# Even weight pieces through six places between two decoder layers, and two more key chunks parked in PSUM

## The chip, the cores and the metric

The kernel runs on one core of a Trainium2 chip. Its time is the device time of one execution in microseconds; the median of several executions is given. The profile is of one further execution.

## What is computed

Two layers, each an attention block over a cached sequence and a small mixer with an MLP, for two sequences (B = 2) with one new token each. In short:

```python
def _A_ref(x, k_cache, v_cache, wq, wo):        # H = 32 heads, Dh = 128, Sk = 16384
    q = heads(x @ wq)
    p = softmax(einsum("bhqd,bhkd->bhqk", q, k_cache) * Dh ** -0.5)
    return merge(einsum("bhqk,bhkd->bhqd", p, v_cache)) @ wo
def _B_ref(x, w1, w2, w3, w4):                  # D = 576, F = 4608; one token, so the shifts give zeros
    x1 = x + hs
    return x1 + gelu(layernorm(x1) @ w3) @ w4
x = x + _A_ref(layernorm(x), K, V, wq, wo)
x = x + _B_ref(layernorm(x), w1, w2, w3, w4)
# and both lines once more
```

Both layers use the same caches and weights. All inputs are bf16.

## The kernel before

**Tiles and places.** The keys and the values of one (sequence, head) pair, a unit, are 4 MB each: 128 partitions with 128 blocks of 128 elements. There are 64 units. A buffer `mem` holds six slots of 4 MB; `Store` (line 269) keeps which 128-byte-per-partition cells of it are in use. `plan` (line 278) appends a transfer with its place to one list; `pump` (line 286) issues the head of the list as soon as its cells have no owner, and stops at the first whose cells are still owned. `release` (line 322) frees the cells of a used piece and pumps again. So all transfers stand in one order on SP's queue, each waits there for the last reader of its place, and one that waits holds back all behind it. SP issues every transfer from line 101.

**A unit.** Half of a unit's key blocks go through PE: eight blocks at a time (a chunk) are transposed into one of four PSUM buffers `tps` (`transposes`, line 1219), copied by ACT to SBUF (`evacuate`, line 1233, instruction at line 1237) and multiplied with q as eight matmuls of one column (`scores`, line 1240, matmuls at line 1251). The other half goes through DVE (`dots`, lines 1271 and 1275), which needs q spread over the partitions (`q_broadcast`, line 1187). The softmax takes its maximum over the partitions on POOL (`softmax_max`, line 1278) and its exponentials on ACT (`softmax_exp`, line 1294); `pv` (line 1327) multiplies the values, 32 blocks at a time. Two loops of three units per turn hold most of it; the stretches around the loops are written out.

**Between the layers.** The last two units of layer 0 (62 and 63) stay in their slots, since layer 1 begins with them: four of the six slots. Their blocks that went through DVE in layer 0 are transposed in place while the weights come in, a chunk at a time, so that layer 1 can score them without a transpose: `turn` (line 1058) transposes a chunk, `settle` (line 1068) has ACT copy it back. Sixteen chunks are turned: four at the start of the last unit (line 967), ten at the places listed in `TURNS` (line 344), two after the w3 product. The unit before them, 61, also stays in part: `park` (line 1073) transposes its first three key chunks (`PARKED`) into the three SBUF buffers `kt`, which frees their place, and the first 72 of its 128 value blocks (`GONE`) are given up and loaded again for layer 1.

The weights wo, w3, w4 and the next wq, some 20 MB, come through what is free: four places of 4608 bytes per partition in the slot of unit 61's values (`A`, lines 524 to 542) and one in the slot of its keys (`B`), where the three parked chunks were. A place holds a piece of 576 KB. Most pieces are of that size; rows 1 and 2 of w3 (by blocks of 128 rows) are 1152 KB in two neighbouring places, the first of wq is 1024 KB, and w4 has two of 288 KB. `rows_projection` (line 859, matmuls at line 872) multiplies wo and w4 piece by piece, `cols_chunk` (line 740, matmuls at line 751) and `cols_tail` (line 759, line 768) w3 and wq; each frees its piece and then turns chunks as `TURNS` says, and `turn` settles them at once unless told otherwise.

Between the products stand the residual sum (line 850), two layernorms (line 684: totals over the partitions by a matmul at line 695, a square root on ACT at line 707, the reciprocal at line 711), the spreading of the last rows (line 725), the GELU (line 909) and the layernorm ahead of wq. The first product of w3 and of wq takes the unnormalized x and is corrected afterwards, so it doesn't wait for the layernorm; the later ones need `xn`.

After q (line 814) `carried` (line 1083) writes out the first three units of layer 1: scores of units 62 and 63 straight from `mem` (`still`), those of unit 61 from the parked chunks (`third`) and from fresh transposes (`fresh`), with dots, maxima and value products between them. Behind the weights the list has the value blocks of unit 61 given up before (four pieces of 576 KB), the keys of unit 0 in quarters, as those of unit 62 are scored, and then whole tiles.

Of the kernel before, what the change touches and what calls it, by code (L numbers as in the profile page):

```python
# [328 lines left out]
class KB:  # L329
# [100 lines left out]

    def plan_tile(self, t, u, slot, cuts=()):

        b, hh = u % self.B, u // self.B
        src = (self.K if t == "k" else self.V)[b, hh].rearrange("(p j) d -> p (j d)", p=128)
        cuts = [0, *cuts, self.NB]
        for a, z in zip(cuts[:-1], cuts[1:]):
            self.plan_piece(t, u, slot, src, a, z - a)

    def plan_piece(self, t, u, slot, src, a, n):
        sem = f"tile{slot}" if n == self.NB else f"piece{slot}_{a}_{n}"  # L440
        self.store.plan((t, u, a, n), sem, slot * self.TILE + 256 * a, 256 * n,
                        [(lambda m: m, src[:, a * 128:(a + n) * 128])])
# [60 lines left out]
    def plan_all(self):  # L503

        T, U, n = self.TILE, self.U, self.KT - 1
        row, w3r, wqr = 2 * self.D, 2 * self.F, 2 * 128 * self.H
        H, MT = self.H, self.MT
# [4 lines left out]
        tiles = self.tile_order(0)  # L512
# [3 lines left out]
        for (t, u), slot in zip(tiles, place):  # L516
# [15 lines left out]
        h = MT // 2  # L532
# [3 lines left out]
        h = H // 2  # L536
# [7 lines left out]
        tiles = self.tile_order(1)  # L544
        place = [(3, 4, 5, 0, 2, 1)[i % 6] for i in range(len(tiles))]
        for i, (t, u) in enumerate(tiles):
            if (t, u) != ("v", third):
                self.plan_tile(t, u, place[i], (quarter, half, half + quarter) if i == 0 else
                               (half,) if i == len(tiles) - 1 else ())
        self.cuts["wo", 1] = [(0, 11, 2 * T), (11, 22, 2 * T + 11 * row), (22, 32, 0)]  # L550
# [188 lines left out]

    def cols_chunk(self, w, l, k, out, pk, n, rhs, rk, cols, first, last=False):  # L740

        c = rhs.shape[-1]
        for i, (kk, lo, hi, _) in enumerate(self.parts[w, l]):
            if kk != k:
                continue
            nm = (w, l, i)
            buf = self.store.buf(nm)

            def f(pe, buf=buf, lo=lo, hi=hi):
                for m in range(lo, hi):  # L750
                    ins = pe.matmul(out[:, m * c:(m + 1) * c], lhsT=cols(buf, m, lo), rhs=rhs, start=first and m == 0,
                                    stop=last, skip_group_check=True)
# [41 lines left out]
    def q_projection(self, l):  # L794
# [6 lines left out]
        self.layernorm("x", self.x, self.xn, "xn",  # L801
                       after=lambda: self.cols_chunk("wq", l, 0, acc, [ak], n, self.raw[:, 0, 0:w], "raw", cols, True, True))
        be = self.coef[:, 1, :]
# [55 lines left out]
    def rows_projection(self, w, l, rhs, rk):  # L859
# [4 lines left out]
        for i, (a, b, _) in enumerate(cuts):  # L864
# [11 lines left out]
            self.store.release(nm)  # L876
            if l == 0:
                self.turn(self.TURNS.get((w, i), 0))

    def z_projection(self, l):  # L880
# [5 lines left out]
        cols = lambda buf, m, lo: self.cols4(l, buf, m)  # L886
        chunk = lambda k: self.cols_chunk("w3", l, k, acc, [ak], MT, self.raw[:, k, :], "raw", cols, k == 0, k == R - 1)
        chunk(0)
        self.layernorm("x1", self.x1, self.xn, "xn", after=lambda: chunk(1))
        self.spread_tail()  # L890
        al, be = self.coef[:, 0, :], self.coef[:, 1, :]
# [55 lines left out]
    def attention(self, l):  # L947
# [11 lines left out]
        for s in range(self.CARRY + 1 if l else 0, U):  # L959
# [6 lines left out]
            still = self.still(l, s)  # L966
            if still and s == U - 1:
                self.unturned = [(v, b) for v in o[U - self.CARRY:] for h in range(2)
                                 for b in range(h * self.BP + self.PB, (h + 1) * self.BP, self.CH)]
                self.unsettled = []  # L970
                self.turn(4)
            self.landed(l, "k", u, both=turning)
            after = self.early(l, s - 1)
            for c in range(2 * n):
# [24 lines left out]
                elif s >= 1:  # L999
# [5 lines left out]
                    if turning or s < U - 1:  # L1005
                        if c == n:
                            self.softmax_exp(l, s - 1, o[s - 1])
# [20 lines left out]
        if leave < U:  # L1028
            self.park(o[leave - 1])
        self.softmax_exp(l, s, u)  # L1030
# [41 lines left out]

    def park(self, u):

        n = self.PARKED
        self.store.carve(("k", u, 0, self.NB), [self.CH * (i + 1) for i in range(n)] + [self.BP])
        for c in range(n):
            self.transposes(0, u, c * self.CH, c, self.chunk)
            self.store.release(("k", u, c * self.CH, self.CH))
            self.unsettled.append((self.chunk, (None, self.kt[c][:, :, :].rearrange("p j n -> p (j n)"), [("kt", c)])))  # L1080
            self.chunk += 1

    def carried(self, o):
# [13 lines left out]
        def fresh(c):  # L1097
            self.transposes(1, o[2], c * self.CH, c, self.chunk)
            self.evacuate(c, self.chunk, (None, self.kt[c % self.NKT][:, :, :].rearrange("p j n -> p (j n)"),
                                          [("kt", c % self.NKT)]))  # L1100
            self.chunk += 1

# [16 lines left out]
        fresh(5)  # L1119
        still(1, 6, 11)  # L1120
        third(4)
        fresh(6)
        still(1, 11, N)
        self.softmax_max(1, 1, o[1])
        third(5)
        fresh(7)
        for g in range(2):
            self.pv(1, 0, o[0], g)
        third(6)
        dots(2)  # L1130
        for g in range(2, 4):
            self.pv(1, 0, o[0], g)
        third(7)
        self.softmax_exp(1, 1, o[1])
        dots(3)
        self.keep_o(1, 0)
        self.keep_l(1, 0)
        for g in range(4):
            self.pv(1, 1, o[1], g)
        self.q_broadcast(o[3], 3)  # L1140
# [300 lines left out]
```

## Time and profile before

| | |
|---|---|
| median of 3 runs | 2559.52 us (2559.41 to 2559.8) |
| the profiled execution | 2557.7 us |
| its span, from the first to the last instruction | 2556.0 us |
| busy: PE, DVE, ACT, POOL | 63%, 74%, 47%, 2% of the span |
| moved by DMA | 1093.19 MB, mean 428 GB/s |

The profile's page gives busy shares for 40 equal slices of the span, the chain of work that ended last, and the groups of instructions by line. Other views give the same for stretches (`from:to length, busy time of each engine with its instructions, granted clock, DMA share, GB/s`), the chain in order of time (`start, us, what`), the timeline (`start, us, engine line operation, in brackets the idle time before and who ended it`) and, for a line that issues transfers, the time from issue to landing. All times are microseconds from the start of the span.

### The profile page before, as it was taken

The page shows a single profiled execution, that of the slowest core. Times are in us where ns is not written, and L with a number is a line of the kernel's source. Part 1 is how long each engine was busy: PE and PEld are TensorE (multiplying, and loading weights), DVE is VectorE, ACT ScalarE, POOL GpSimd, SP SyncE. Part 2 cuts the span into 40 slices and gives each one's busy share as a digit, 9 for nine tenths or more (in the row PEclk, how much of TensorE's full clock was granted, in tenths as well). Part 3 has the DMA queues.
Part 4 walks back from the last instruction along what each step waited for, and adds up shares of the span by engine and source line. Part 5 has one row for each costly group of instructions (what it writes and reads, how often), then busy time and mean ns, then how long its engine had stood idle before and what let it go on. Part 6 is the DMA issues. An engine that isn't in the chain of part 4 may idle for free.

```text
span 2556.0 us, 74895 instructions
## 1 busy us (share of the span) xinstructions
PE 1616.7 (63%) x34407; PEld 1582.5 (62%) x34407; DVE 1899.1 (74%) x2074; ACT 1200.7 (47%) x1808; POOL 52.5 (2%) x151
## 2 busy tenths in 40 slices
PE   4666666666666666665777666666666666666566
PEld 3666666656656666665667656666665666666566
DVE  5877777777777777777648777777777777777774
ACT  3544444544444454444435544454444445444442
POOL 0000000000000000000000000000000000000000
PEclk8555555555555555555655555555555555555655
DMA  9999999999999999999999999999999999999999
GB/s 410 430 430 433 431 431 432 432 431 431 432 431 432 431 432 433 431 432 432 414 359 427 433 431 431 433 431 432 432 430 434 430 432 433 431 431 432 431 433 388
DMA packets 46496, 1093.19 MB, mean 428 GB/s; under 512 B 5092, under 2 KB 6248, under 8 KB 11624
## 3 DMA queue, kind: packets, MB, share of 16 engines
q1 hardware_dynamic: 46440, 1092.40, 99.9%
q8 instruction: 41, 0.67, 0.1%
q14 instruction: 15, 0.12, 0.0%
HBM read 1092.37 MB, written 0.00 MB: 427 GB/s over the span
## 4 chain that ended last, share of the span: by engine, by line
DMA 66%; DVE 22%; PE 5%; issue 5%; SPq 1%; ACT 1%; DVEq 0%; POOLq 0%
DMA mem<-in_A_k_cache_dram 64%; DVE s_dve L1275 12%; DVE prod L1271 8%; PE tps L1225 2%; PE mps L1345 2%; DMA mem<-in_B_w_dram 2%; SPq L101 1%; PE sps L1251 1%; DMA mem<-in_A_wq_dram 1%; PE sps L1196 1%; ACT mem L1237 0%; DVE diag L1192 0%; DMA mem<-in_A_wo_dram 0%; DVE q_col L1189 0%; DVE l L1323 0%
## 5 line engine op out<-in xcount | busy, mean ns | idle before, releaser
L1237 ACT ACTIVATE kt<-tps 128x1024 bf16<-128x1024 bf16 x992 | 1003.0, 1023 | 878.4 <-PE tps L1225 862.0
L1275 DVE TENSOR_REDUCE s_dve<-prod 128x16 f32<-128x2048 bf16 x504 | 1152.1, 2286 | 17.3
L1225 PE MATMUL tps<-ident,mem 128*128 128x128 bf16 x8192 | 1000.2, 300 | 140.1 <-POOLq L202 134.8
L1271 DVE TENSOR_TENSOR prod<-mem,qb 128x2048 bf16<-128x2048 bf16 x504 | 616.7, 1224 | 533.1 <-POOLq L202 498.1
L1345 PE MATMUL mps<-p,mem 128*128 128x1 bf16 x16384 | 512.1, 165 | 549.6 <-POOLq L202 522.5
L1225 PEld LDWEIGHTS tps<-ident,mem 128*128 128x128 bf16 x8192 | 762.7, 136 | 149.8 <-POOLq L202 144.3
L1345 PEld LDWEIGHTS mps<-p,mem 128*128 128x128 bf16 x16384 | 488.2, 105 | 557.3 <-ACT p L1306 553.7
L1251 PEld LDWEIGHTS sps<-q_col,kt 128*128 128x128 bf16 x7936 | 399.6, 113 | 0.7 <-issue 0.5
L1251 PE MATMUL sps<-q_col,kt 128*128 128x1 bf16 x7936 | 387.8, 170 | 0.6 <-issue 0.4
L1196 PE MATMUL sps<-diag,ones_bf 128*128 128x128 bf16 x127 | 36.5, 288 | 194.1 <-DVE diag L1192 194.1
L1196 PEld LDWEIGHTS sps<-diag,ones_bf 128*128 128x128 bf16 x127 | 13.3, 105 | 204.3 <-DVE diag L1192 204.3
L1300 ACT ACTIVATE mx<-mx 128x1 f32<-128x1 f32 x128 | 26.1, 204 | 233.6 <-POOL mx L1291 233.6
L1199 ACT ACTIVATE qb<-sps 128x128 bf16<-128x128 f32 x127 | 35.2, 277 | 139.2 <-PE sps L1196 139.2
L1291 POOL PARTITION_ALL_REDUCE mx<-mx x128 | 50.1, 392 | 2450.7 <-DVE mx L1289 2321.5
L1237 ACT ACTIVATE mem<-tps 128x1024 bf16<-128x1024 bf16 x32 | 31.3, 1043 | 33.1 <-PE tps L1225 28.0
L1303 ACT ACTIVATE p<-s_dve,mx 128x64 bf16<-128x64 f32 x126 | 43.8, 348 | 4.1
L1306 ACT ACTIVATE p<-sps,mx 128x64 bf16<-128x64 f32 x128 | 37.7, 294 | 0.1
L1286 DVE TENSOR_REDUCE mx<-sps 128x1 f32<-128x64 f32 x128 | 27.6, 216 | 7.5 <-PE sps L1251 7.5
L872 PE MATMUL mps<-prod,mem 128*128 128x2 bf16 x680 | 22.1, 166 | 17.2 <-DMA mem<-in_B_w_dram 7.0
L872 PEld LDWEIGHTS mps<-prod,mem 128*128 128x128 bf16 x680 | 20.2, 104 | 19.5 <-DMA mem<-in_B_w_dram 7.8
L1192 DVE TENSOR_SCALAR diag<-ident,q_f 128x128 bf16<-128x128 bf16 x127 | 31.1, 245 | 0.0
L707 ACT ACTIVATE misc<-misc 128x2 f32<-128x2 f32 x8 | 2.4, 294 | 52.4 <-DVE misc L705 52.4
(122 smaller groups left out, 293.1 us busy)
## 6 DMA issues: line engine op xcount, KB each, us to landing
mem<-in_A_k_cache_dram SPq DMA_DIRECT2D x124, 4096.0 KB, 40.7
mem<-in_A_v_cache_dram SPq DMA_DIRECT2D x123, 4096.0 KB, 49.6
mem<-in_B_w_dram SPq DMA_DIRECT2D x9, 1152.0 KB, 33.4
mem<-in_B_w_dram SPq DMA_DIRECT2D x17, 576.0 KB, 7.3
mem<-in_A_v_cache_dram SPq DMA_DIRECT2D x3, 2048.0 KB, 40.4
mem<-in_A_wq_dram SPq DMA_DIRECT2D x5, 1024.0 KB, 7.0
mem<-in_A_wo_dram SPq DMA_DIRECT2D x8, 576.0 KB, 18.6
mem<-in_A_wq_dram SPq DMA_DIRECT2D x8, 512.0 KB, 6.9
```

The lines of the kernel that those rows point to most:

```text
L872: ins = pe.matmul(self.mps[:, t * B:(t + 1) * B], lhsT=buf[:, o:o + 128], rhs=rhs(k), start=(k == 0 and t == 0), stop=(k == last), skip_gr ...
L1196: self.pe(lambda pe: pe.matmul(qps, lhsT=self.ones_bf[:, :], rhs=self.diag[:, :], start=True, stop=True, skip_group_check=True), reads=["o ...
L1199: self.act(lambda e: e.activation(out=self.qb[i][:, :], in_=qps, func=ACT.Copy), reads=[("qps", i)], writes=[("qb", i)], sig=("qb", i))
L1225: ins = pe.transpose(self.tps[t][:, j * 128:(j + 1) * 128], buf[:, j * 128:(j + 1) * 128], self.ident[:, :])
L1237: self.act(lambda e: e.activation(out=out, in_=self.tps[t][:, :], func=ACT.Copy), reads=[("tps", t)], writes=keys, sig=("evac", c, t, k))
L1251: ins = pe.matmul(self.sps[sp][:, c * self.CH + j:c * self.CH + j + 1], lhsT=buf[:, j * 128:(j + 1) * 128], rhs=self.q_col[:, sp:sp + 1], ...
L1271: self.dv(lambda e: e.tensor_tensor(out=prod, in0=buf.rearrange("p (j d) -> p j d", d=128), in1=qbc, op=ALU.mult), reads=[("qb", r)] + key ...
L1275: self.dv(lambda e: e.tensor_reduce(out=sd[:, c0:c0 + DB], in_=prod, axis=AX.X, op=ALU.add), reads=["prod"], writes=[("s_dve", r)], sig=(" ...
L1291: self.pool(lambda e: e.partition_all_reduce(mx[3], mx[2], channels=128, reduce_op=ROP.max), reads=[("mx2", i)], writes=[("mx3", i)])
L1303: self.act(lambda e: e.activation(out=p[:, n:self.NB], in_=self.s_dve[i][:, 0:self.NB - n], func=ACT.Exp, bias=mx[4], scale=self.scale, ac ...
L1306: self.act(lambda e: e.activation(out=p[:, 0:n], in_=self.sps[i][:, 0:n], func=ACT.Exp, bias=mx[4], scale=self.scale, accum_out=self.ls[:, ...
L1345: ins = pe.matmul(self.mps[:, 448:449], lhsT=buf[:, j * 128:(j + 1) * 128], rhs=p[:, col:col + 1], start=b == 0, stop=b == self.NB - 1, sk ...
```

## The change

1. **Six places, even pieces.** `PARKED` is 5. The two new parked chunks are transposed behind the second wo product and stay in two of the four PSUM buffers until layer 1 copies them; `self.full` names these buffers and `turn` and `fresh` pass over them. Their place in `mem` makes a second place `c[1]` beside `B`, now `c[0]`. All pieces of wo, w3, w4 and wq go through the six places in turn, and w3 and wq are cut into halves: w3 comes in nine pieces (seven before), wq in nine (eight before).
2. **Turns.** The four chunks that were turned at the start of the last unit are turned in the middle of the one before it. Of the ten in `TURNS` some stand behind other products. Chunks turned inside a layernorm (after the second w3 row and the first wq row) are settled only when the layernorm has been issued (`held`).
3. **The list behind the weights.** The first quarter of unit 0's keys goes to the place of the parked chunks instead of unit 62's slot and stands ahead of the last of unit 61's value pieces.
4. **Layer 1's first products.** In `carried` both units' scores come in a row; the dots, maxima, fresh transposes and value products follow in another order. Fresh transposes 3 and 4 drop out, since these chunks wait in PSUM.

```diff
-    PARKED = 3
+    PARKED = 5
-    TURNS = {("w3", 0): 1, ("w3", 1): 1, ("w3", 2): 1, ("w3", 3): 1, ("w4", 1): 1, ("w4", 4): 1, ("w4", 7): 1,
-             ("wq", 1): 1, ("wq", 2): 1, ("wq", 3): 1}
+    TURNS = {("w3", 0): 1, ("w3", 1): 1, ("w3", 2): 1, ("w4", 1): 1, ("w4", 3): 1, ("w4", 6): 1, ("w4", 8): 1,
+             ("wq", 0): 1, ("wq", 1): 1, ("wq", 2): 1}
...
-        A, B = [4 * T + P * i for i in range(4)], T
-        assert 256 * self.GONE == 4 * P and 256 * 8 * self.PARKED >= P
-        self.cuts["wo", 0] = [(4 * i, 4 * i + 4, at) for i, at in enumerate((*A, B, *A[:3]))]
+        a, c = [4 * T + P * i for i in range(4)], [T, T + P]
+        assert 256 * self.GONE == 4 * P and 256 * 8 * self.PARKED >= 2 * P and 256 * 8 * self.NKT >= P
+        turn = iter([*a, c[0]] + [a[0], a[1], c[1], a[2], a[3], c[0]] * 6)
+        h = MT // 2
+        self.cuts["wo", 0] = [(i, i + 4, next(turn)) for i in range(0, 32, 4)]
+        halves = lambda n: [(k, m, z, next(turn)) for k in range(self.KT - 1) for m, z in ((0, n), (n, 2 * n))] + \
+                           [(self.KT - 1, 0, 2 * n, next(turn))]
+        w3 = halves(h)
...
-        self.cuts["w4", 0] = [(h + a, h + b, at) for h in (0, MT // 2)
-                              for a, b, at in zip(g[:-1], g[1:], (A[2], A[3], B, A[0], A[1]))]
+        self.cuts["w4", 0] = [(h * i + p, h * i + q, next(turn)) for i in range(2) for p, q in zip(g[:-1], g[1:])]
...
-        self.plan_cols("w3", 0, self.w3, [(0, 0, h, A[3]), (0, h, MT, B), (1, 0, MT, A[0]), (2, 0, MT, A[2]),
-                                          (3, 0, h, B), (3, h, MT, A[0]), (4, 0, MT, A[1])])
+        self.plan_cols("w3", 0, self.w3, w3)
...
-        self.plan_cols("wq", 1, self.wq, [(0, 0, H, A[2]), (1, 0, h, B), (1, h, H, A[1]), (2, 0, h, A[0]),
-                                          (2, h, H, A[2]), (3, 0, h, A[3]), (3, h, H, B), (4, 0, H, A[1])])
+        self.plan_cols("wq", 1, self.wq, halves(H // 2))
...
-        for i in (0, 2, 3, 1):
-            self.plan_piece("v", third, 4, self.V[b, hh].rearrange("(p j) d -> p (j d)", p=128), i * self.GONE // 4,
-                            self.GONE // 4)
+        for i in (1, 2, 3, None, 0):
+            if i is None:
+                self.plan_piece(*tiles[0], T, self.K[b2, h2].rearrange("(p j) d -> p (j d)", p=128), 0, quarter)
+            else:
+                self.plan_piece("v", third, 4 * T, self.V[b, hh].rearrange("(p j) d -> p (j d)", p=128),
+                                i * self.GONE // 4, self.GONE // 4)
...
-            self.turn(self.TURNS.get((w, k), 0))
+            self.turn(self.TURNS.get((w, k), 0), settle=not held)
...
             if l == 0:
+                if (w, i) == ("wo", 1):
+                    self.park(self.order(0)[self.U - self.CARRY - 1], self.NKT, self.PARKED)
                 self.turn(self.TURNS.get((w, i), 0))
...
         self.layernorm("x1", self.x1, self.xn, "xn", after=lambda: chunk(1))
+        if l == 0:
+            self.settle()
...
         for _ in range(n):
             u, b = self.unturned.pop(0)
+            while self.chunk % self.NT in self.full:
+                self.chunk += 1
             self.transposes(0, u, b, 0, self.chunk)
...
-    def park(self, u):
+    def park(self, u, a, z):
+        if a == 0:
+            self.store.carve(("k", u, 0, self.NB), [self.CH * (i + 1) for i in range(self.PARKED)] + [self.BP])
+        for c in range(a, z):
             self.transposes(0, u, c * self.CH, c, self.chunk)
             self.store.release(("k", u, c * self.CH, self.CH))
+            if c < self.NKT:
+                self.unsettled.append((self.chunk, self.chunk_place(c)))
+            else:
+                self.full = (*self.full, self.chunk % self.NT)
             self.chunk += 1
...
         still(0, 4, N)
+        dots(0)
+        self.softmax_max(1, 0, o[0])
+        still(1, 0, N)
+        self.softmax_exp(1, 0, o[0])
         for c in range(3):
             third(c)
-        dots(0)
-        self.softmax_max(1, 0, o[0])
+        dots(1)
+        self.softmax_max(1, 1, o[1])
         fresh(3)
         fresh(4)
-        still(1, 0, 6)
-        self.softmax_exp(1, 0, o[0])
-        dots(1)
+        for g in range(2):
+            self.pv(1, 0, o[0], g)
         third(3)
         fresh(5)
...
```

More of the change, by code (lines that the diff above doesn't have):

```diff
@@ L548, in plan_all @@
                 self.plan_tile(t, u, place[i], (quarter, half, half + quarter) if i == 0 else
-                               (half,) if i == len(tiles) - 1 else ())
+                               (half,) if i == len(tiles) - 1 else (), 0 if i else quarter)
         self.cuts["wo", 1] = [(0, 11, 2 * T), (11, 22, 2 * T + 11 * row), (22, 32, 0)]
@@ L738, in unscaled, with cols_chunk @@
                 reads=["x", "raw"], writes=["raw"])
-    def cols_chunk(self, w, l, k, out, pk, n, rhs, rk, cols, first, last=False):
+    def cols_chunk(self, w, l, k, out, pk, n, rhs, rk, cols, first, last=False, held=False):
         c = rhs.shape[-1]
@@ L966, in attention @@
             still = self.still(l, s)
[L967 to L971, printed above, removed]
             self.landed(l, "k", u, both=turning)
@@ L1006, in attention @@
                         if c == n:
+                            if still:
+                                self.unturned = [(v, b) for v in o[U - self.CARRY:] for h in range(2)
+                                                 for b in range(h * self.BP + self.PB, (h + 1) * self.BP, self.CH)]
+                                self.unsettled, self.full = [], ()
+                                self.turn(4)
                             self.softmax_exp(l, s - 1, o[s - 1])
@@ L1028, in attention @@
         if leave < U:
-            self.park(o[leave - 1])
+            self.park(o[leave - 1], 0, self.NKT)
         self.softmax_exp(l, s, u)
@@ L1097, in fresh @@
         def fresh(c):
[L1098 to L1101, printed above, removed]
+            if c >= self.PARKED:
+                while self.chunk % self.NT in self.full:
+                    self.chunk += 1
+                self.transposes(1, o[2], c * self.CH, c, self.chunk)
+                at, self.chunk = self.chunk, self.chunk + 1
+            else:
+                at, self.full = self.full[0], self.full[1:]
+            self.evacuate(c, at, self.chunk_place(c))
         def third(c):
@@ L1127, in carried @@
         for g in range(2):
-            self.pv(1, 0, o[0], g)
+            self.pv(1, 1, o[1], g)
         third(6)
-        dots(2)
         for g in range(2, 4):
-            self.pv(1, 0, o[0], g)
+            self.pv(1, 1, o[1], g)
         third(7)
-        self.softmax_exp(1, 1, o[1])
         dots(3)
[L1136 to L1139, printed above, removed]
         self.q_broadcast(o[3], 3)
```

36 lines of the change are left out of this document (20 added, 16 removed).

## The prediction

> **What bounds the kernel now.** I read the page first, then the stretches between the layers, then the chain of waits and the timeline inside them.
>
> ```profile
> GB/s 410 430 430 433 431 431 432 432 431 431 432 431 432 431 432 433 431 432 432 414 359 427 433 431 431 433 431 432 432 430 434 430 432 433 431 431 432 431 433 388
> HBM read 1092.37 MB, written 0.00 MB: 427 GB/s over the span
> DMA 66%; DVE 22%; PE 5%; issue 5%; SPq 1%; ACT 1%; DVEq 0%; POOLq 0%
> ```
>
> The kernel is bound by its transfers: in nearly every slice the queue moves 430 to 433 GB/s, and only the first, the last and two slices in the middle (414, 359) fall short. The middle two are the way from layer 0 to layer 1. Outside the ends, the only time to be had is there. The stretches of that way (columns: length, each engine's busy time and instructions, clock, DMA share, GB/s):
>
> ```profile
> 1262.00:1266.00 4.00, 3.41 (x104) 3.21 (x101) 1.94 (x6) 2.34 (x3) 0.00 (x0) 0.50 1.04 417
> 1266.00:1275.00 9.00, 4.67 (x140) 4.20 (x140) 0.01 (x1) 0.00 (x0) 0.00 (x0) 0.50 0.97 381
> 1275.00:1290.00 15.00, 9.65 (x194) 8.78 (x194) 6.38 (x41) 3.55 (x5) 0.00 (x0) 0.50 0.91 329
> 1290.00:1303.00 13.00, 9.58 (x196) 8.81 (x194) 2.27 (x13) 6.63 (x8) 0.00 (x0) 0.50 0.95 333
> 1303.00:1322.00 19.00, 10.69 (x242) 9.74 (x240) 3.92 (x24) 5.79 (x7) 0.00 (x0) 0.50 0.96 348
> 1322.00:1338.00 16.00, 14.84 (x434) 14.75 (x432) 10.38 (x8) 7.64 (x14) 2.50 (x2) 0.50 1.01 405
> 1410.00:2500.00 1090.00, 690.12 (x14501) 677.65 (x14499) 833.10 (x843) 525.02 (x788) 19.70 (x56) 0.57 1.00 432
> ```
>
> From 1275 to 1322 us no engine is busy for more than 75% of a stretch, and the queue moves 329 to 348 GB/s. In 1262 to 1266, when weight pieces of 576 KB land from a full queue, it moves 417. So the pieces are not slow; too few are under way. The chain of waits in 1266 to 1322 says why:
>
> ```profile
> 1274.31 0.71 PE mps L872 x20
> 1275.02 0.02 issue
> 1275.03 6.68 DMA mem<-in_B_w_dram
> ...
> 1281.76 1.34 PE sps L751 x36
> ...
> 1283.12 6.27 DMA mem<-in_B_w_dram
> ...
> 1297.18 6.75 DMA mem<-in_B_w_dram
> 1303.93 0.05 issue
> 1303.97 0.71 PE mps L872 x20
> 1304.68 0.02 issue
> 1304.70 6.68 DMA mem<-in_A_wq_dram
> ```
>
> It is a round: a product frees a place, 0.02 us later a transfer into it is issued, 6.3 to 6.8 us later it lands, its product runs 0.7 us and frees the next. Five places can hold only five pieces per round. The same line's transfers, first all 31 issued in 1266.5 to 1321, then a lone late pair and the lone first piece of wq:
>
> ```profile
> DMA to landing us min/median/max: 4.8/6.7/7.9
> DMA to landing us min/median/max: 4.8/5.7/6.6
> DMA to landing us min/median/max: 7.0/7.0/7.0
> ```
>
> **What the change is worth, part by part.**
>
> *Six even places.* A piece of 589,824 B takes 1.41 us at 417 GB/s. A new transfer keeps the queue full only if enough is still to land when it is issued. How much is bounded by the last fence: 4.8 less its own 1.41 is 3.4 us; the 1024 KB piece gives 7.0 less 2.5, 4.5 us. I take 4.2, near the upper end, since the chain's transfers (6.3 to 6.8 us) stand nearer to it. With five places a freed place finds four pieces ahead, 4 x 1.41 = 5.64 us, less 0.7 us for the product that ran first: 4.9. The product may be late by only 0.7 us before the queue starves; a 1152 KB piece (w3 rows 1 and 2) fills two places, which makes it worse. With six it is 5 x 1.41 - 0.7 = 6.35, and 2.15 us of lateness are free.
>
> How late are products that wait for other things than their weights?
>
> ```profile
> 1275.74 0.69 PE L872 MATMUL mps<-prod,mem 128*128 128x2 bf16 x20 [0.74 <-DMA mem<-in_A_wo_dram]
> 1278.21 1.31 PE L751 MATMUL sps<-misc,mem 128*128 128x7 bf16 x36
> 1279.38 1.01 PE L1225 MATMUL tps<-ident,mem 128*128 128x128 bf16 x8
> 1280.73 0.59 PE L695 MATMUL mps<-misc,ones_f 128*128 128x4 f32 x2 [0.34 <-DVE misc L692]
> 1285.23 0.17 DVE L711 RECIPROCAL misc<-misc 128x2 f32<-128x2 f32 x1 [3.25 <-ACT misc L707]
> 1285.85 0.21 PE L725 MATMUL mps<-xn,sel 128*128 128x2 bf16 x2 [1.89 <-DVE xn L715]
> ...
> 1291.25 0.71 PE L768 MATMUL sps<-xt,mem 128*128 128x4 bf16 x18
> 1294.54 1.23 PE L872 MATMUL mps<-prod,mem 128*128 128x2 bf16 x40 [0.85 <-DVE prod L915]
> 1305.38 1.12 PE L872 MATMUL mps<-prod,mem 128*128 128x2 bf16 x30
> 1307.82 0.59 PE L695 MATMUL mps<-misc,ones_f 128*128 128x4 f32 x2 [1.33 <-DVE misc L692]
> ```
>
> After wo the first w3 product starts 2.5 us after the last wo product, whose successor lands 1.41 later: 1.1 us late. The next (behind L695 at 1280.73, so from 1281.2) starts 3.0 later while two pieces take 2.8: 1.3 late. After GELU w4 starts 3.3 us after the tail: 1.9 late. The first wq product can start 0.5 after L695, 2.9 after the last w4 product began, of which the landing takes 1.2: at most 1.7 late. All fit into 2.15 and none into 0.7.
>
> *The settled order.* The L711 row's 3.25 us is the second layernorm's square root standing behind a copy of a turned chunk on ACT. The held settle puts the root first. With it xn comes some 3 us earlier, and w3's third product is bound by the 1.24 + 0.88 us of product and turn ahead of it, under 1 us late; without it it would be over 3 us late, past even the new limit.
>
> *The sum.* Against a full queue: 15 x (1 - 329/417) = 3.17, 13 x (1 - 333/417) = 2.62, 19 x (1 - 348/417) = 3.14: 8.9 us. The 9 x (1 - 381/417) = 0.8 us of 1266 to 1275 stays, since the first wo product still waits for attention's end and the sixth place is first used by the eighth piece. I leave 1.4 us for the two delays near the limit (GELU, wq), where 4.2 may be short by 0.3 and the queue then needs a piece or two to fill. Gain 7.5.
>
> *Layer 1's first products.* Line 1251 frees the tile of the second carried unit only after interleaved work:
>
> ```profile
> 1321.28 0.22 DVE L814 TENSOR_TENSOR q_f<-sps,prod 128x64 f32<-128x64 f32 x1 [5.77 <-PE sps L768]
> 1322.70 2.75 PE L1251 MATMUL sps<-q_col,mem 128*128 128x1 bf16 x96
> 1334.00 0.67 PE L1251 MATMUL sps<-q_col,mem 128*128 128x1 bf16 x19 [1.16 <-issue]
> ```
>
> Its 4 MB successor is issued 13.4 us after q; with both units' 256 products in a row it is 0.5 + 256 x 0.029 = 7.9 us. The three earlier quarters still land then, so 16 x (1 - 405/432) = 1.0 us of the 1322 to 1338 stretch goes: **8.5 us in all**. The count of rounds agrees: 31 pieces of the new cut from the sixth on are 6.2 rounds of five or 5.2 of six, one round of 7.5 us (6.75 + 0.75) less, and the 1.0.
>
> *At nothing:* Two more parked chunks are 16 transposes, 1.8 us of PE (0.9 per chunk, as between 1279.38 and the next) behind the second wo product. Queued behind them are the wo products; PE waits there anyway, and they leave layer 1's two fresh transposes out again. Without that cover they cost 1.8. The four turns that move one unit earlier (3.5 us of PE) delay the places of the first four wo pieces, which land 28 to 30 us after their issue:
>
> ```profile
> DMA to landing us min/median/max: 28.4/29.0/29.7
> ```
>
> SP issues three transfers more, nine pieces of w3 for seven and nine of wq for eight; a piece takes 1.41 us to move and, as the chain shows, under 0.1 to send off once its place is free. The quarter of k0 that goes ahead of the last v piece only changes the order of a queue that is filled either way. In layer 1 the dots, maxima and value products are the same instructions in another order. The sixth place is there in time: two wo products (0.7 each) and two parked chunks (0.9 each) after attention's end, 3.2 us, while the three pieces ahead of the eighth take 4.2.
>
> The Trainium skill, "DMA: Bandwidth & Descriptors", section Bandwidth, says that transfers should be batched to 1 MiB or more to get 75% of the peak, which speaks against halving the 1152 KB pieces. The trace disagrees while others are under way: 417 against 432 GB/s, 97%, in pieces of 576 KB. By the rule the halves would move no faster than the pieces do now, and the gain would be nil; that is the first rival.
>
> **The rivals.** *Depth does not help* (no change): what sets the rate between the layers is the size of a piece or the chain of layernorm, GELU and turns, so that a sixth piece only waits longer. For it: landing times reach 7.9 us, and every delay above is past 1 us. If the need were 5.35 us instead of 4.2, the free lateness would be 1.0 and five delays would overflow by 0.1 to 0.9, with refilling 4 to 5 us; gain 4, 2553.7, and nil, 2557.7, if piece size rules (2555.5 and 2559.5 as medians). Against: 417 GB/s in the same pieces.
>
> *Two transpose buffers starve the turns* (slower): the parked chunks hold two of the four PSUM buffers from the second wo product to layer 1, so each turn waits until the copy of the turn before last is made.
>
> ```profile
> L1237 ACT ACTIVATE mem<-tps 128x1024 bf16<-128x1024 bf16 x12 | 12.1, 1021 | 25.6 <-PE tps L1225 20.6 <-PE mps L725 5.0
> L914 ACT ACT_TABLE_LOAD x1 | 1.3, 1283 | 0.0
> ```
>
> A copy behind a table load costs a turn up to 1.28 + 1.02 = 2.3 us, and every weight product queued behind the turn on PE is late by it. Beyond the free 2.15 it decides; twelve turns at 2.3 would add 27.6, and half of that, 13.8, less the 8.5, gives 2563 (median 2564.8). Against: ACT stands idle 25.6 us before those twelve copies, waiting for PE.
>
> *All of it comes back:* the queue never starves, 0.8 and 1.4 go too and q's earlier tiles help the next ones: 12 us, 2547.5.
>
> **How the numbers follow.** The sum is made against the profiled execution (2557.7; span 2556.0): 2549.2. The median of the runs shown is 2559.52, 1.82 above it, so 2551.0. Forecast (gain 5.2 to 11) 0.72; all comes back 0.08; depth does not help 0.14, taken as within 0.2% (5.1 us, about what a measurement of this kernel can tell from no change); buffers starve 0.06. The range runs from 13 us of gain (2546.5: the 10.7 us of loss in all five stretches and some later) to 3 us (2556.5: the need at its worst). It leaves out the nil end of "depth does not help", the starved buffers and a sliver below, under 0.2.
>
> **What would show it.** Right: 400 GB/s or more in each stretch between the layers, transfers all but gone as links of the chain there, landings at over 7 us in the median (a longer queue), the L711 idle time gone, the first 4 MB tile of layer 1 issued about 8 us after q. Wrong: 340 GB/s as before with landings at 8 us (depth does not help), or PE waiting for ACT ahead of L1225's successor (buffers). A second loss that the sum lacks would be new idle time in the loop of layer 1, since nothing but 432 GB/s stands there now.

## The result and the profile after

The changed kernel takes 2550.51 us (median of 7 runs, 2550.26 to 2552.05), the kernel before 2559.48 beside it (7 runs, 2559.38 to 2561.85): a ratio of 0.9965, 95% interval 0.9953 to 0.9976, 9.0 us or 0.35% less. The forecast was 2551.0, in a range from 2546.5 to 2556.5.

The page of the changed kernel, first its line of GB/s in 40 slices, then the memory's total, then the chain that ended last by engine:

```profile
GB/s 410 427 432 432 432 432 432 432 432 431 432 432 433 430 433 430 433 430 433 418 409 428 433 431 432 432 432 432 432 432 432 432 432 431 432 431 432 432 432 374
HBM read 1092.37 MB, written 0.00 MB: 428 GB/s over the span
DMA 66%; DVE 22%; issue 5%; PE 5%; SPq 1%; another core or an unknown queue 0%; ACT 0%; DVEq 0%; POOLq 0%; POOL 0%
```

The same bytes are read. The slice that stood at 359 is at 409. The stretches of the way between the layers, cut at the same times as before (the last column is GB/s):

```profile
1266.00:1275.00 9.00, 5.76 (x146) 5.24 (x143) 0.00 (x0) 0.00 (x0) 0.00 (x0) 0.50 1.00 391
1275.00:1290.00 15.00, 11.41 (x223) 10.77 (x224) 7.68 (x49) 4.78 (x7) 0.00 (x0) 0.50 1.01 402
1290.00:1303.00 13.00, 10.03 (x222) 9.23 (x219) 1.08 (x6) 5.97 (x8) 0.00 (x0) 0.50 1.01 399
1303.00:1322.00 19.00, 12.64 (x347) 11.90 (x348) 9.12 (x29) 7.30 (x11) 1.25 (x1) 0.50 1.00 397
1322.00:1338.00 16.00, 9.90 (x289) 9.51 (x287) 8.27 (x8) 5.05 (x10) 1.25 (x1) 0.50 1.05 442
1410.00:2500.00 1090.00, 688.90 (x14479) 676.37 (x14478) 835.88 (x848) 525.97 (x793) 20.04 (x57) 0.57 1.00 432
```

329, 333 and 348 GB/s have become 402, 399 and 397, and the loop of layer 1 stands at 432 as before: nothing was given back there. The transfers and the longest waits for nothing shown that are left in the chain of waits between 1266 and 1322 us:

```profile
1269.49 6.15 DMA mem<-in_A_wo_dram
...
1279.50 7.52 DMA mem<-in_B_w_dram
...
1294.03 6.97 DMA mem<-in_B_w_dram
...
1306.97 6.95 DMA mem<-in_A_wq_dram
...
1319.81 1.96 issue
```

Four transfers stand in it (six before), with 49% of that stretch of the chain (72% before). So the way still holds rounds of "free a place, wait for its piece", one for each of four stops. By the records of landing, the last piece of wq lands at 1313.91 us instead of 1320.54 (6.6 us earlier) and the first 4 MB tile of layer 1 at 1340.77 instead of 1348.24 (7.5 earlier); that distance holds to the last few tiles.

The profiled pair differs by less than the medians: 2557.7 - 2552.05 = 5.65 us. 2552.05 is the slowest of the changed kernel's 7 runs, 1.5 above their median (its last tile lands only 5.9 us earlier than before's, one step of 1.6 us lost near the end), while the profiled execution of before was 1.8 below its median: 5.65 + 1.54 + 1.78 = 8.97.

### The profile page after: what moved, and what is told of

It is laid out like the page before. It is cut to its first block, busy times and chain, and to the rows that moved or that the text cites. A ratio compares the mean times of both kernels' runs of the same rounds, so it can differ in the third digit from the quotient of the medians.

```text
span 2550.2 us, 74899 instructions
## 1 busy us (share of the span) xinstructions
PE 1617.0 (63%) x34407; PEld 1582.7 (62%) x34407; DVE 1899.4 (74%) x2074; ACT 1201.8 (47%) x1808; POOL 53.5 (2%) x151
## 4 chain that ended last, share of the span: by engine, by line
DMA 66%; DVE 22%; issue 5%; PE 5%; SPq 1%; another core or an unknown queue 0%; ACT 0%; DVEq 0%; POOLq 0%; POOL 0%
DMA mem<-in_A_k_cache_dram 64%; DVE s_dve L1300 12%; DVE prod L1296 8%; PE mps L1370 2%; PE tps L1250 2%; DMA mem<-in_B_w_dram 2%; SPq L101 1%; PE sps L1276 1%; PE sps L1221 0%; DVE diag L1217 0%; DMA mem<-in_A_wq_dram 0%; DVE l L1348 0%; DVE mx L1311 0%; DVE q_col L1214 0%
```

## The experiments

Theory A is the prediction's: what slows the weights is the number of pieces under way; a product may be late by a free margin before the queue starves, and six places raise that margin. The rivals of the first four: B, the even cut is what helps; C, the held settle is; D, the new order of layer 1's first products is. From e5 on the letters B and C mean what the expectation says beside them. The twelve kernels ran in three sets, the changed kernel in another, and the kernel before stood at 2559.5, 2560.0 and 2559.9 us in the three; so differences of the medians below some 0.5 us aren't told apart here. Beside the median I use a sum from the traces, the *loss by landings*: the time from the landing of w3's first piece to that of wq's last, less the 35.4 us that these bytes take at 417 GB/s. It is 8.1 us in the kernel before and 1.5 in the changed one; e4, which is the same up to q, shows 0.9, so single executions differ by some 0.6.

**e1: five places, all else as changed** (and what hangs on the place: the quarter of k0 goes back behind the value pieces, and chunks 3 and 4 are not parked but transposed afresh in layer 1).

```diff
-    PARKED = 5
+    PARKED = 3
...
-        a, c = [4 * T + P * i for i in range(4)], [T, T + P]
+        a, c = [4 * T + P * i for i in range(4)], [T]
...
+        turn = iter([*a, c[0]] * 8)
```

> The changed kernel with the sixth place taken out: even pieces of 576 KB and 512 KB through five places, three chunks parked as before; settled order and layer 1's order as changed. Theory A (the number of pieces under way sets the rate; with five places a product may be only 0.7 us late, with six 2.15): the five late products of 1.1 to 1.9 us overflow by 0.4 to 1.2 each, about 4 us, so half of the gain goes: 2554 to 2556 us. Rival B (even cut alone carries the gain): 2550.5. Rival C (the settled order alone carries the gain): 2550.5 to 2551.

2555.79 us (11 runs, 2554.17 to 2557.68; ratio 0.9988, 0.9979 to 0.9997). Its stretches:

```profile
1275.00:1290.00 15.00, 10.41 (x214) 9.66 (x212) 6.83 (x45) 3.66 (x5) 0.00 (x0) 0.50 0.99 364
1290.00:1303.00 13.00, 9.61 (x205) 8.72 (x203) 1.85 (x11) 6.57 (x8) 0.00 (x0) 0.50 0.97 364
1303.00:1322.00 19.00, 12.52 (x315) 11.76 (x316) 5.29 (x26) 7.61 (x10) 0.00 (x0) 0.50 0.99 357
```

With the same pieces, the same held settles and the same order of products, but five places, all three stay near 360 GB/s. The sixth place, with what hangs on it, is worth 5.3 us, and the loss by landings is 5.2 us instead of 1.5: theory A.

**e2: six places, pieces cut as before** (w3's rows 1 and 2 and wq's row 0 whole again, in two neighbouring places).

```diff
-        w3 = halves(h)
+        w3 = [(0, 0, h, a[2]), (0, h, MT, a[3]), (1, 0, MT, c[0]), (2, 0, MT, a[0]), (3, 0, h, a[2]), (3, h, MT, a[3]),
+              (4, 0, MT, c[0])]
...
```

> Six places, but the pieces cut as before: rows 1 and 2 of w3 whole (1152 KB in two neighbouring places) and the first of wq whole (1024 KB). Theory A: a whole row waits for two places and can be used only when all of it has landed, 1.4 us later, so three products come 1.4 us later than in the changed kernel; with 2.15 us free this costs 1 to 3 us: 2551.5 to 2553.5. Rival B (the even cut carries the gain): 2557 to 2559.5. Rival C (settled order): 2550.5.

2553.63 us (11 runs, 2552.8 to 2554.73; ratio 0.9979, 0.997 to 0.9988). The stretch that holds w3 and the one after it:

```profile
1275.00:1290.00 15.00, 10.15 (x198) 9.47 (x199) 6.64 (x43) 3.67 (x5) 0.00 (x0) 0.50 0.91 340
1290.00:1303.00 13.00, 9.88 (x208) 8.95 (x208) 2.03 (x12) 6.74 (x8) 0.00 (x0) 0.50 0.98 379
```

The stretch of w3 falls to 340, almost to its old 329, the next one to 379 from 399: a 1152 KB piece holds two places and waits until both are free (the first was issued at 1276.37, with 2.0 us of transfers still to land). The even cut is worth 3.1 us beside the sixth place, a little more than A said, far less than B; the loss by landings is 4.8 us.

**e3: the settles not held**, neither in the second layernorm nor in the one ahead of wq.

```diff
-            self.turn(self.TURNS.get((w, k), 0), settle=not held)
+            self.turn(self.TURNS.get((w, k), 0))
```

> The changed kernel, but every turned chunk is settled at once, ahead of the layernorm's square root on ACT. Theory A: xn of the second layernorm comes 3 us later again, the third row of w3 is then over 3 us late, past the free 2.15 by about 1.1, and with the refilling 1 to 2.5 us are lost: 2551.5 to 2553; the idle time ahead of the reciprocal is 3 us again. Rival C (the settled order carries the gain): 2557 to 2559.5. Rival B: 2550.5.

2553.56 us (11 runs, 2552.92 to 2554.6; ratio 0.9977, 0.9968 to 0.9986): 3.05 us lost, 0.6 past A's upper end. The reciprocals of the second layernorm and of the one ahead of wq, in this kernel and then in the changed one (start, length, idle time before it and its releaser):

```profile
1284.58 0.17 DVE L716 RECIPROCAL misc<-misc 128x2 f32<-128x2 f32 x1 [2.65 <-ACT misc L712]
...
1309.43 0.17 DVE L716 RECIPROCAL misc<-misc 128x2 f32<-128x2 f32 x1 [4.14 <-ACT misc L712]
```

```profile
1282.23 0.17 DVE L716 RECIPROCAL misc<-misc 128x2 f32<-128x2 f32 x1 [0.28 <-ACT misc L712]
...
1305.73 0.17 DVE L716 RECIPROCAL misc<-misc 128x2 f32<-128x2 f32 x1 [0.28 <-ACT misc L712]
```

The wait on ACT is there with the copy ahead of the root and gone without it: with the hold `xn` comes 2.35 us earlier in the second layernorm and 3.7 us earlier ahead of wq. By the trace the first of the two costs nothing: w3's third product runs 2.36 us after its piece has landed, but the last piece of w4 lands at 1301.58 us, and at 1301.72 in the changed kernel. The loss comes behind the second: the last piece of wq lands 0.7 us later than in the changed kernel and the first 4 MB tile 2.1 later (1342.86). So the layernorm ahead of wq is where the hold counts. No run takes back one of the two holds alone.

**e4: layer 1's first products in the old order.**

```diff
         still(0, 4, N)
-        dots(0)
-        self.softmax_max(1, 0, o[0])
-        still(1, 0, N)
-        self.softmax_exp(1, 0, o[0])
         for c in range(3):
             third(c)
...
```

> The changed kernel with layer 1's first products in the old order (scores of the second carried unit interleaved with dots, fresh transposes and maxima). Theory A: only the 1.0 us of the stretch after q comes back: 2551.5. Rival D (layer 1's order carries the gain, since DVE and PE start earlier on it): 2556 or more.

2551.55 us (7 runs, 2551.16 to 2552.22; ratio 0.997, 0.9959 to 0.9982): 1.04 us lost, A's value, though the two kernels' runs overlap (the changed kernel's reach 2552.05). The trace has the place, the stretch behind q:

```profile
1322.00:1338.00 16.00, 11.84 (x362) 11.72 (x362) 9.65 (x13) 3.90 (x8) 1.60 (x2) 0.50 0.90 362
```

362 GB/s here against 442 with the new order; the first 4 MB tile is issued 4.6 us later (1329.01) and lands 1.7 later.

**e5 and e6: 1.0 us of lateness added ahead of w4's first product** (0.9 by the traces), with six places and with five. 32 small products whose result nobody reads stand there; nothing is left out.

```diff
+        if l == 0:
+            def late(pe):
+                for _ in range(self.LATE):
+                    ins = pe.matmul(self.mps[:, 384:388], lhsT=self.sel[0][:, :], rhs=self.gT[:, 0:4], start=True, stop=True)
+                return ins
+            self.pe(late, reads=["prod", "sel0"], writes=["mps"])
```

> The changed kernel with 32 more small products on TensorE (some 1.0 us in all, into spare columns of mps, read by nobody) between layer 0's GELU and the first product of w4, so that w4's first piece is used about 1.0 us later. Theory A (a piece may be late by the free lateness, 2.15 us with six places, and costs only what lies beyond it): in the changed kernel w4's first piece landed at 1290.02 and was used at 1291.38, 1.36 late; 2.36 is past 2.15 by 0.2, so the time goes from 2550.5 to 2550.7, at most 2551.0. Rival B (the chain of compute sets the end, and lateness passes straight through): +1.0, 2551.5.

> The same 1.0 us of lateness ahead of w4's first product, in the kernel with five places and even pieces (2555.79). Theory A: with five places only 0.7 us are free and the first piece of w4 is later than that already, so all of the 1.0 us shows: 2556.8. Rival B (lateness counts the same whatever the number of places): the same increase as in the kernel with six places. Rival C (w4's pieces were not what bounds the stretch with five places): no increase.

Six places: 2550.91 us (5 runs, 2550.76 to 2551.14; ratio 0.9965, 0.9952 to 0.9979), 0.4 more than the changed kernel. Five: 2555.71 (11 runs, 2554.22 to 2557.81; ratio 0.9986, 0.9977 to 0.9995), the same as e1. So lateness does not pass straight through, as a bound by the compute chain (B) would have it; with six places the medians say so only narrowly (B's 2551.5 is 0.6 away), with five by 1.1. But with five places A failed as it was put: it said 1.0 and got nothing. The trace shows why. In e1 the pieces ahead had been delayed already: w4's first piece landed at 1291.97, 1.95 later than in the changed kernel, and its product was only 0.65 late. And the piece that e6 issued late, at 1293.94, when 2.1 us of transfers were still to land, landed at 1298.00, 0.54 us after a full queue would have: a need of 2.6 us, where the prediction had taken 4.2.

**e9 and e10: the same with 3.0 us** (`LATE = 96`; by the traces 2.6 us, from 1291.44 to 1294.02 in e9).

> The changed kernel with 96 of the small products ahead of w4's first product, 3.0 us in place of 1.0. Theory A with the prediction's 2.15 us of free lateness: 1.36 + 3.0 - 2.15 = 2.2 us more than the changed kernel, 2552.7 (where 1.0 gave 0.4). Rival B (compute sets the end): +3.0, 2553.5. Rival C (this place never bounds): 2550.5 to 2551.

> The same 3.0 us in the kernel with five even places, where 1.0 us cost nothing (2555.7 against 2555.8). In its trace w4's first piece landed 0.65 us before its use. Theory A with a fixed need of 4.2 us (0.7 free): 2.95 more, 2558.7. Theory A with a need that is shorter at this place (the piece issued 2.1 us before the landing ahead of it still landed only 0.5 late, a need of 2.6, so 2.3 us free): 0.65 + 3.0 - 2.3 = 1.4 more, 2557.1. Rival C: no increase, 2555.8.

Six places: 2553.74 us (8 runs, 2552.44 to 2554.87; ratio 0.9975, 0.9964 to 0.9985), 3.2 more. Five: 2558.3 (11 runs, 2556.12 to 2560.55; ratio 0.9992, 0.9983 to 1.0001), 2.5 more than e1. The stretch of w4 in each, e9 first:

```profile
1290.00:1303.00 13.00, 10.89 (x286) 10.19 (x285) 1.03 (x6) 5.67 (x7) 0.00 (x0) 0.50 0.91 331
```

```profile
1290.00:1303.00 13.00, 11.43 (x284) 10.73 (x283) 1.94 (x12) 6.01 (x8) 0.00 (x0) 0.50 0.79 295
```

By the medians the first 0.9 us cost 0.4 and nothing, and the next 1.7 cost 2.8 and 2.6, more than was added; e9's runs range over 2.4 us and e10's over 4.4. By the traces (landing of wq's last piece) the first 0.9 us cost 0.3 and nothing, the next 1.7 cost 1.5 and 2.0. Both say that there is a free margin and that past it lateness costs about its full length. Its size isn't settled by these runs: 1.36 + 2.6 - 3.2 gives 0.8 us for six places by the medians; by the traces (last piece of wq at 1315.77 instead of 1313.91, 1.9 later) it is 2.1, which is A's 2.15. By its median e9 alone would fit B as well.

**e7: the held settle alone, in the kernel before.** Five places, three parked chunks, the old pieces and the old order stay; the edit is the line that e3 takes back, with `held` for the same products and the two `settle` calls ahead of the layernorms' rest. But this kernel turns no chunk behind wq's first product (`TURNS`), so the hold ahead of wq holds nothing here, and e7 tests the second layernorm alone.

> The kernel before with the held settle alone: five places, three parked chunks, the uneven pieces and the old order of layer 1's first products stay. By the prediction's step taken alone (xn comes some 3 us earlier, w3's third product is over 3 us late without it and under 1 us with it): up to 2 to 2.5 us gained, 2557. Theory A by the free lateness: two products of that stretch wait for their landings in any case, since with five places and 1152 KB pieces the queue has run empty before the third one, so 0 to 1.0 gained, 2558.5 to 2559.5.

2559.11 us (11 runs, 2558.35 to 2560.88; ratio 0.9997, 0.9988 to 1.0006): no difference that can be told. The reciprocal of the second layernorm comes at 1282.33 us instead of 1285.23, but the first 4 MB tile lands no earlier (1348.89; before 1348.24). The wait that costs most in e3 isn't there to be taken away. The layernorm ahead of wq in the kernel before:

```profile
1309.36 0.17 DVE L711 RECIPROCAL misc<-misc 128x2 f32<-128x2 f32 x1 [0.28 <-ACT misc L707]
```

So e3 and e7 agree on the second layernorm, whose hold is worth nothing that shows. e3's 3.05 us is the price of turning a chunk ahead of wq without a hold, which the kernel before never paid.

**e8: a seventh place**, for 0.59 MB more to move.

```diff
-    GONE = 72
+    GONE = 90
```

> The changed kernel with a seventh place: 90 instead of 72 of the last V tile's 128 blocks of columns go early and come back later, 0.59 MB more to move, 1.4 us at 432 GB/s. Theory A: the 2.0 us that the four stretches still lose against 417 GB/s in the changed kernel fall to 0.5 or less, so the two nearly cancel: 2549.9 to 2550.9. Rival (what is left there does not come from the number of pieces): 2550.5 + 1.4 = 2551.9.

2551.17 us (5 runs, 2550.88 to 2551.33; ratio 0.9966, 0.9952 to 0.998): between A and its rival. The first and the last of its four stretches:

```profile
1266.00:1275.00 9.00, 5.84 (x151) 5.33 (x147) 0.00 (x0) 0.00 (x0) 0.00 (x0) 0.50 1.02 405
...
1303.00:1322.00 19.00, 13.08 (x367) 12.43 (x366) 9.71 (x29) 7.92 (x12) 1.25 (x1) 0.50 1.03 413
```

Against 417 GB/s the stretches from 1266 to 1322 (405, 410, 394, 413) lose 9 x 12/417 + 15 x 7/417 + 13 x 23/417 + 19 x 4/417 = 1.4 us, the changed kernel's (391, 402, 399, 397) 2.6 by the same sum. So by these two executions 1.2 us come back, and 1.4 are paid for the bytes.

**e11 and e12: chunks parked before attention's end; and a turn moved away from wq's first product** (e12 has both).

```diff
+            self.settle()
+            self.park(o[leave - 1], self.NKT, self.PARKED)
...
-                if (w, i) == ("wo", 1):
-                    self.park(self.order(0)[self.U - self.CARRY - 1], self.NKT, self.PARKED)
...
-        turn = iter([*a, c[0]] + [a[0], a[1], c[1], a[2], a[3], c[0]] * 6)
+        turn = iter([*a, *c] * 6)
...
-        for i in (1, 2, 3, None, 0):
+        for i in (0, 1, 2, 3, None):
...
-    TURNS = {("w3", 0): 1, ("w3", 1): 1, ("w3", 2): 1, ("w4", 1): 1, ("w4", 3): 1, ("w4", 6): 1, ("w4", 8): 1,
+    TURNS = {('w3', 0): 1, ('w3', 1): 1, ('w3', 2): 1, ('w4', 1): 1, ('w4', 3): 1, ('w4', 5): 1, ('w4', 6): 1, ('wq', 0): 1, ('wq', 1): 1, ('wq', 2): 1}
```

> The changed kernel with all five chunks parked and copied before attention's end, not two of them behind the second product of wo, so that the sixth place is free some 3 us earlier and the pieces go through the six places in plain order. Theory A (what the four stretches still lose, 2.0 us, comes from too few pieces under way just ahead of wo's and w3's products): 0.5 to 1.5 us less, 2549.0 to 2550.0. Rival: nothing left to gain there, or the extra transposes delay attention's end: 2550.5 to 2552.3.

> The same, and the turn that stands between w4's ninth piece and the first product of wq moved to the sixth piece, so that wq's first product, the late one, starts about 0.9 us earlier. Theory A: another 0.3 to 0.9 us, 2548.3 to 2549.7. Rival: as with the chunks alone, or slower since the turn now delays w4.

2550.38 us (5 runs, 2550.03 to 2551.12; ratio 0.9961, 0.9948 to 0.9975) and 2549.96 (5 runs, 2549.72 to 2550.31; ratio 0.9959, 0.9945 to 0.9973). Both lie above what A said. Chunks parked early bring nothing that can be told (the rival); e12 is the lowest median of all, 0.55 below the changed kernel's, but from another set of runs and hardly past what can be told. Its stretches of w4 and wq (e11, without the moved turn, has 398 and 412 there):

```profile
1290.00:1303.00 13.00, 10.17 (x222) 9.21 (x220) 2.02 (x13) 8.00 (x9) 0.00 (x0) 0.50 1.02 390
1303.00:1322.00 19.00, 13.59 (x377) 12.85 (x378) 8.91 (x23) 5.79 (x10) 1.25 (x1) 0.50 1.03 416
```

## Why the prediction was right

**The bound and the place** were right: the gain lies where the queue fell short. Undoing the sixth place, the even cut, the held settle or the new order costs 5.3, 3.1, 3.05 and 1.04 us. That is 12.5 in all for a change worth 9.0, but e3's part isn't a step back towards the kernel before (see e7), and without it the sum is 9.4. So the runs don't show that the parts spoil each other. Of the signs that the prediction named, some came only in part: 402, 399 and 397 GB/s, but 391 in the first stretch; four transfers as links of the chain and not "all but gone"; the idle time ahead of the second layernorm's reciprocal went from 3.25 to 0.28 us as said.

**Six even places, 7.5 us.** In the profiled pair the last piece of wq lands 6.6 us earlier. The three stretches lose 15 x 15/417 + 13 x 18/417 + 19 x 20/417 = 2.0 us against 417 GB/s, where 1.4 was left over; by landings the loss went from 8.1 to 1.5. So the mechanism was right and this term 0.6 to 0.9 too large. By the landing intervals of the changed kernel from wo's seventh piece on, four losses above 0.25 us remain. Two are the late products that the sum named: a piece of w4 behind GELU (1.69 us instead of 1.42), and the seventh piece of wq (2.10 instead of 1.25), whose place was freed by the first wq product, 1.67 us late. There the sum's 5 x 1.41 was too much. The pieces ahead were smaller (one of 288 KB, or five of 512 KB), so 4.35 and 4.0 us were still to land, where 6.35 less the lateness gives 5.0 and 4.7. The other two have 4.9 us still to land and are none of the sum's: the seventh piece of wo (2.45 instead of 1.42), and the first quarter of k0 behind wq (4.04 instead of 2.48, landing at 1322.20). In all fourteen kernels one of wo's last pieces lands 1.0 to 1.5 us late, with 3.6 to 5.5 us still to land, five places or six.

**The lateness after GELU** was put at 1.9 us. w4's first piece landed at 1290.02, and its product

```profile
1291.38 1.23 PE L879 MATMUL mps<-prod,mem 128*128 128x2 bf16 x40 [0.41 <-DVE prod L926]
```

is 1.36 late: inside the margin, as predicted, by more than predicted.

**The need of 4.2 us** as one number is the weak step. Over the profiled executions of all fourteen kernels I put each weight or value piece issued from 1266 to 1320 us (473 of them) into a class by what was still to land when it was issued, and took its landing interval less its bytes at 417 GB/s:

```
still to land, us   pieces   mean loss, us   over 0.4 us
under 3                 14            1.12           93%
3 to 4.5                59            0.50           49%
4.5 to 6               231            0.08            7%
6 and more             169            0.03            2%
```

From 4.5 us up the queue is as good as full in most cases; below, the loss sets in by degrees and not at a point, with needs from 2.2 to over 5 for single pieces. So 4.2 was near the place where the loss sets in, but it isn't a limit from which lateness can be reckoned to tenths, and e6's forecast failed by that.

**The settled order** is the step that failed in part. It was said to bring `xn` of the second layernorm some 3 us earlier; it is 2.35. Without it w3's third product was to be over 3 us late, past the new limit. In e3 it is 2.36 late, a piece is issued into its place with 4.0 us still to land, and the queue loses nothing. What the hold is worth in time, 3.05 us, lies by e3's trace behind the layernorm ahead of wq, of which the prediction's step says nothing: without the hold the root and its table load (1.28 us) stand behind the copy there, and `xn` comes 3.7 us later.

**Layer 1's first products, 1.0 us**: 1.04 in e4, and in the profiled pair 7.5 - 6.6 = 0.9 by the landings. But the first 4 MB tile was issued at 1324.37, 9.7 us after q, and not 7.9. The row between, on PE:

```profile
1321.77 2.57 PE L1276 MATMUL sps<-q_col,mem 128*128 128x1 bf16 x91 [1.96 <-issue]
```

Without these 1.96 us of idle time it is 7.8. The product count was right; the stall was not foreseen (below).

**At nothing** held. The turns did not starve on two PSUM buffers: all the copies of turned chunks between 1266 and 1314 us,

```profile
L1262 ACT ACTIVATE mem<-tps 128x1024 bf16<-128x1024 bf16 x12 | 12.2, 1021 | 13.6 <-PE tps L1250 11.7 <-PE mps L730 1.9
```

found ACT idle and waiting for PE, 13.6 us in all, and no idle time of PE ahead of these transposes was ended by ACT. **Depth does not help** is out by e1 and the stretches. On this the Trainium skill, "DMA: Bandwidth & Descriptors", section Bandwidth, asks for transfers of 1 MiB or more to reach 75% of the peak; the trace disagrees again: the changed kernel's pieces of 512 and 576 KB move at 397 to 402 of 432 GB/s, 92 to 93%, and the stretch with e2's pieces of 1152 KB at 340.

**The check named for landings** (over 7 us in the median) came out on the line: 7.0 for all of SP's transfers between 1266.5 and 1316 us.

```profile
DMA to landing us min/median/max: 5.5/7.0/9.0
```

**The step from the profile to the median** was right by chance in part: I took the changed kernel's median to lie 1.82 above its sum as before's did. But the scatter of the runs shrank with the losses: in the sets above, the kernel before ranges over 4 to 5 us and e1, e6 and e10 over 3.5 to 4.4 (e7 2.5), the changed kernel over 1.8 and e4, e5, e8, e11 and e12 over 0.4 to 1.1 (e2, e3 and e9 1.7 to 2.4; the smallest ranges are of sets of five runs, before's of 18 to 29). The sum itself, 2549.2, is 1.1 below the fastest run, 2550.26; the two errors nearly cancel. In the profiled pair the 4 MB tiles of layer 1 land 7.4 us earlier, where the sum said 8.5. That the median came within 0.5 us of the forecast is luck to that extent.

## What to carry to other kernels

Where a stream comes through few places, count what is still to land when a place is freed (here 4.5 us were enough, 3 were not) and set it against how late the consumer can be; a further place, smaller even pieces and an earlier consumer all help with that. Count the pieces that are really ahead, each by its size. And before the price of taking an edit out (e3) is set beside the gain of putting it in alone (e7), see that both kernels have the wait that it removes; here one of the two waits exists only in the changed kernel. Once the queue is full to within a few per cent, more depth that has to be paid with bytes returned no more than it cost (e8).

## What the runs showed that I had not expected

PE's idle time "waiting for nothing that the profile shows" goes with the loading of instructions. In the window 1319 to 1321.5 us of the changed kernel, in which PE stops at 1319.81, the DMA queues hold one such packet, of 16 KB, which begins at 1319.28 and takes 1.06 us:

```profile
q8 instruction: 1, 0.02, 2.7%
```

The next at 1325.16 and 1325.41 stand at a gap of 2.64 us that begins at 1325.32. In both cases PE goes on 1.43 us after the 16 KB packet's end. In e5, e8, e11 and e12 the same two gaps (1.6 to 2.0 and 2.6 to 2.9 us) stand at the same packets. Products of 0.03 us in a row (133 in 3.73 us ahead of the first gap) use up instructions fastest, and that is where the gaps are. That the packet's arrival ends the gap is read from their times; no run took it away.

Losses of 1.0 to 1.6 us appear now and then with a full queue, as at 1381.16 us, where a 4 MB tile landed 11.25 us after the one before instead of 9.71, with 11.6 us still queued. The trace has 16 landing records for each transfer, and I count it as landed with the last; so a packet of instructions that holds up one of the DMA engines could be the cause. The times fit: of the 400 pieces in the table with 4.5 us or more still to land, 152 landed within 3.5 us of the start of a 16 KB instruction packet, and 18 of them lost over 0.4 us; of the other 248, 3 did. The 3.5 us were chosen with these times in view, most packets go with no loss, and no run moved or removed a packet: the cause is not shown.
